# One more rounded chunk pair, its low part on GpSimd: a change to a fused attention and feed-forward kernel

## The chip, the cores and the metric

The kernel runs on one core of one Trainium2 chip. The metric is device time in microseconds (us) of one execution; lower is better. The engines of the core are named as the profile names them: PE (TensorE, matmuls), PEld (its weight loads), DVE (VectorE), ACT (ScalarE), POOL (GpSimd) and SP (SyncE, which here issues every DMA).

## The reference

Two stages in f32. First an attention through 49 "agents" per batch (4 batches of 12480 tokens, width 128): every agent takes a softmax over all keys and gathers values, then every token takes a softmax over the agents and gathers those. Then a feed-forward layer on the 49920 token rows that come out:

```python
h = x @ w_in            # 128 -> 2048
g = h - np.tanh(h)
return (g @ w_out)      # 2048 -> 128
```

## The kernel before

Tokens are cut into 100 blocks of up to 500 (the last of each batch has 480), 25 to a batch. The 2048 hidden columns are cut into 16 chunks of 128, taken two at a time: a block has 8 *chunk pairs*, i = 0 to 7, and one chunk pair of one block is a *step*. Two neighbouring blocks form a *block pair* of 16 steps; the step's place in it is its *position*, `pos = n % 2 * 8 + i`, 0 to 15. There are 800 steps in 50 block pairs, and nearly all the time goes into them.

A step consists of

- the first product on PE (`m1`, line 563): six matmuls into a PSUM tile h. The attention output is never formed; its 49 rows are folded into w_in beforehand;
- on ACT, y = tanh(h) (line 573) and z = a scaled square of y (line 578). Since h is small, h - tanh(h) is taken as h times that square;
- on DVE, the product g = h * z (`mul`, line 583), 128 x 1000, from PSUM and SBUF into SBUF;
- the second product (`m2`, line 632), which adds g times w_out into a PSUM tile acc of the block. It has two forms. The *plain* form multiplies g as f32 with an f32 copy of the weights (`wo_f`). The *rounded* form splits g in two numbers of the faster matmul type: GpSimd rounds it to gh (`high`, line 613), DVE subtracts to get the low part gl = g - gh (`low`, line 618), and PE does gh with the low weights, gh with the high weights and gl with the high weights, 12 matmuls of 500 columns in six pairs of row halves.

`PLAIN = (1, 3, 7, 8, 9)` lists the positions with the plain form; the first block is all plain. So 545 steps are rounded and 255 plain.

The order of the work on each engine is the order in which it is recorded (lines 850 to 915, `issue_order`): in step k come product k on DVE and its rounding on POOL; tanh and square of step k+1; the first product of step k+2; the low part of step k-1 (`low(1)` keeps one back); and the second product of step k-1 (`out`). An engine does its instructions strictly in that order. Position 2 also begins by closing the previous block: ACT copies half of acc to o (line 644), DVE adds the other half (line 641). The tiles g, gh and gl rotate over 4, 3 and 3 buffers; h, acc and small PSUM tiles share four double banks.

Between the steps lie smaller jobs. Each block pair prepares the token softmax of the next (lines 508 to 552). In the first three batches the first product over keys and values of the next batch (`phase1`) is handed out piece by piece from the queue `kq`: 13 score jobs, two for the maximum, 13 value jobs (marked by the table `VS`, starting at positions 1 and 8), then the rest. A value job has a subtraction on GpSimd (line 344).

After a block pair's second block is closed, one DMA of up to 1000 columns stores both (line 809).

Of the kernel before, what the change touches and what calls it, by code (L numbers as in the profile page):

```python
# [12 lines left out]
F32 = mybir.dt.float32  # L13
# [6 lines left out]
ALU = mybir.AluOpType  # L20
# [38 lines left out]
KV = 3  # L59
VB = 4  # L60
PLAIN = (1, 3, 7, 8, 9)
NB = dict(y=2, z=2, g=4, gh=3, gl=3)
Q0 = 2
NV = 10
# [9 lines left out]
VS = {1: 1, 8: 2}  # L74
# [4 lines left out]
def width(n):  # L79
    return min(BLK, N - n % NBLK * BLK)  # L80


def column(n):
    return n // NBLK * N + n % NBLK * BLK
# [18 lines left out]
class Build:  # L103
# [31 lines left out]
    def constants(self):  # L135
# [17 lines left out]
        self.wo_l = c.tile([128, NCH, C], F32R, tag="wo_l", name="wo_l")  # L153
        self.wo_f = {i: c.tile([128, 2 * C], F32, tag=f"wo_f{i}", name=f"wo_f{i}") for i in sorted({i % 8 for i in PLAIN})}
        self.vb = [c.tile([128, GT, C + 2], F32, tag=f"v{i}", name=f"v{i}") for i in range(VB)]
# [47 lines left out]
    def load_w_out(self, c, raw):  # L203
        one, two = self.wtile("gl", NB["gl"]), self.wtile("gh", NB["gh"])
        cut = lambda t, k: t[:, 512 * k : 512 * (k + 1)]
        return self.decode(raw, self.wf[:, c * 512 : (c + 1) * 512], cut(one, 0), cut(one, 1), cut(two, 0), cut(two, 1))
# [364 lines left out]
    def tanh(self, h, w):  # L571
        y = self.wtile("y", NB["y"])[:, : 2 * w]
        self.nc.scalar.activation(self.pair(y), h, AF.Tanh, scale=TSC)  # L573
        return y

    def square(self, y):
        z = self.wtile("z", NB["z"])[:, : y.shape[1]]
        self.nc.scalar.activation(z, y, AF.Square, scale=GSC)  # L578
        return z

    def mul(self, h, z, w):
        g = self.wtile("g", NB["g"])[:, : 2 * w]
        self.nc.vector.tensor_tensor(self.pair(g), h, self.pair(z), ALU.mult)  # L583
        self.mul_at = self.last_name()
        return g

    def act_general(self, hv, w):
        nc = self.nc
        d = self.wtile("y", NB["y"])[:, : 2 * w]
        u = self.wtile("z", NB["z"])[:, : 2 * w]  # L590
        nc.scalar.activation(self.pair(d), hv, AF.Tanh)
# [21 lines left out]
        self.nc.gpsimd.tensor_scalar(gh, g, 1.0, 0.0, ALU.mult, ALU.add)  # L613
        return gh

    def low(self, g, gh):
        gl = self.wtile("gl", NB["gl"])[:, : g.shape[1]].bitcast(F32R)
        self.nc.vector.tensor_tensor(gl, g, gh.bitcast(F32), ALU.subtract)  # L618
        return gl

    def m2(self, acc, i, gh, gl, wf=None):
        nc = self.nc
        w = gh.shape[1] // 2
        high, low = (lambda c: self.wo_h[:, 2 * i + c, :]), (lambda c: self.wo_l[:, 2 * i + c, :])
        if gl is None:
            terms = [(lambda c: wf[:, c * C : (c + 1) * C], gh, c) for c in range(2)]
        else:
            terms = [(low, gh, 0), (high, gh, 0), (low, gh, 1), (high, gh, 1), (high, gl, 0), (high, gl, 1)]
        for k, (weights, g, c) in enumerate(terms):
            for r in range(2):  # L630
                rows = slice(HALF * r, HALF * (r + 1))
                nc.tensor.matmul(  # L632
                    acc[:, r, :w],
                    weights(c)[rows],
                    g[rows, c * w : (c + 1) * w],
                    start=i == 0 and k == 0,
                    stop=i == NCH // 2 - 1 and k == len(terms) - 1,
                )
# [46 lines left out]
    def fast(self):  # L685
        nc, tc = self.nc, self.tc
        HP = NCH // 2
        blocks = [(b, j) for b in range(B) for j in range(NBLK)]
        steps = [(n, i) for n in range(len(blocks)) for i in range(HP)]
# [100 lines left out]
        kq = []  # L790
        r1, r2, done = [], [], []
# [7 lines left out]
        def out_at(n):  # L799
            first = n - n % 2  # L800
            if n == first and n // 2 not in outs:
                outs[n // 2] = self.work.tile([128, GW], F32, tag="out", name="o", bufs=2)
            return outs[n // 2][:, n % 2 * width(first) :][:, : width(n)]

        def finish(n):
            self.add_up(out_at(n), acc[n])
            if n % 2 == 1:
                w = width(n - 1) + width(n)
                nc.sync.dma_start(self.outT[:, column(n - 1) : column(n - 1) + w], outs[n // 2][:, :w])

# [13 lines left out]
        def product(k):  # L824
            n, i = steps[k]
            g = self.mul(hs.pop(k), zs.pop(k), width(n))
            plain = n == 0 or n % 2 * HP + i in PLAIN
            gh = None if plain else self.high(g)
            r1.append((n, i, g, gh))

        def low(keep):
            while len(r1) > keep:
                n, i, g, gh = r1.pop(0)
                r2.append((n, i, g, None) if gh is None else (n, i, gh, self.low(g, gh)))

        def out(k):
            while r2:
# [12 lines left out]
        for k, (n, i) in enumerate(steps):  # L850
            b = blocks[n][0]
            pos = (n % 2) * HP + i
            p = n // 2
            if n % NBLK == 0 and i == 0 and b + 1 < B:
                kq = self.phase1(b + 1)
            begin = kq[0][0].get(pos, 0) if kq and n else 0
            if done and done[0][1] < k - 1:
                self.take(out_at(done[0][0]), acc[done[0][0]])
                finish(done.pop(0)[0])
            product(k)  # L860
            if n == LATE and i < NP:
                self.bound(0, i, slice(PCUT[i], PCUT[i + 1]))
# [18 lines left out]
            for j in AHEADS.get(pos, (AHEAD,)) if n else (AHEAD,):  # L881
                first_product(k + j)
            low(1)
            mark = self.last_on(ET.DVE)
            if n == 0:
# [16 lines left out]
            for kind in [x[0] for x in kq[:begin]]:  # L902
                if kind is kq[0][0] and kind.get(pos):
                    start(kq.pop(0)[1](pos))
        low(0)
        out(len(steps))
        while done:
            self.take(out_at(done[0][0]), acc[done[0][0]])
            finish(done.pop(0)[0])
# [64 lines left out]
```

## Time and profile before

| | |
|---|---|
| time, 3 runs | 2016.40, 2017.02 (median), 2018.77 us |
| the profiled execution | 2018.59 us |
| its span, first to last instruction | 2016.8 us |
| busy in the span: PE, DVE, ACT, POOL | 1986.9, 1825.6, 1806.5, 999.9 us |
| mean granted TensorE clock | 0.995 of full |

A matmul's row in the profile covers its whole passage through the array, so neighbouring matmuls overlap; what a group of matmuls takes of PE's time is read from the distance between starts. Two matmuls of 64 rows each, on the two halves of the array, run side by side. Line numbers are those of the kernel before; in the changed kernel the same lines stand one further up to the storing of a block, and three to five further behind it.

### The profile page before, as it was taken

How to read it: one execution, taken by the hardware profiler on the slowest of the kernel's cores; microseconds unless marked ns; L12 is line 12 of the kernel's file. 1: busy time of each engine (PE TensorE's matmuls, PEld its weight loads, DVE VectorE, ACT ScalarE, POOL GpSimd, SP SyncE). 2: the span in 40 equal slices, each digit the busy share in tenths (PEclk: the TensorE clock that was granted, in tenths of full speed). 3: DMA queues.
4: the chain of work that ended last, by engine and by line, in shares of the span. 5: the costliest groups of instructions: out<-in, count | busy, mean ns of one | idle time of the engine just before them, and what ended most of it. 6: DMA issues, size and time to landing. Idle time of an engine off the chain costs nothing.

```text
span 2016.8 us, 49577 instructions
## 1 busy us (share of the span) xinstructions
PE 1986.9 (99%) x20779; PEld 1460.9 (72%) x20779; DVE 1825.6 (91%) x1986; ACT 1806.5 (90%) x2052; POOL 999.9 (50%) x702
## 2 busy tenths in 40 slices
PE   8899999999999999999999999999999999999998
PEld 7477767777677777777677777777767777777775
DVE  7799999889999998898999999889899999999997
ACT  3789989899999998899999999998999999999996
POOL 1254455555445455554454454555545546555554
PEclk9899999999999999999999999999999999999999
DMA  9422112221111222221012111221101101101100
GB/s 331 135 85 93 54 45 84 83 61 44 54 61 65 78 71 60 78 75 60 31 36 92 61 58 44 71 61 56 54 29 34 52 31 35 52 29 37 39 24 27
DMA packets 76601, 129.70 MB, mean 64 GB/s; under 512 B 5384, under 2 KB 55376, under 8 KB 76368
## 3 DMA queue, kind: packets, MB, share of 16 engines
q1 hardware_dynamic: 76368, 126.44, 19.2%
q8 instruction: 165, 2.70, 0.6%
q14 instruction: 68, 0.56, 0.1%
HBM read 81.10 MB, written 25.56 MB: 53 GB/s over the span
## 4 chain that ended last, share of the span: by engine, by line
PE 84%; ACT 8%; DVE 4%; issue 2%; DMA 1%; SPq 0%; POOL 0%; DVEq 0%; POOLq 0%
PE acc L632 49%; PE h L563 26%; ACT z L578 4%; ACT y L573 4%; DVE g L583 2%; PE misc L508 2%; PE misc L357 2%; PE pt L538 1%; PE misc L301 1%; PE h L273 1%; DVE gl L618 1%; PE misc L472 1%; DMA v<-w_out 1%; PE h L380 0%; ACT s L349 0%
## 5 line engine op out<-in xcount | busy, mean ns | idle before, releaser
L613 POOL TENSOR_SCALAR gh<-g 128x1000 fp32r<-128x1000 f32 (+1 forms) x545 | 853.0, 1565 | 622.5 <-DVE g L583 578.6
L583 DVE TENSOR_TENSOR g<-h,z 128x1000 f32<-128x1000 f32 (+1 forms) x800 | 955.5, 1195 | 133.5 <-ACT z L578 122.9
L573 ACT ACTIVATE y<-h 128x1000 f32<-128x1000 f32 (+1 forms) x800 | 802.4, 1003 | 68.6 <-PE h L563 60.5
L578 ACT ACTIVATE z<-y 128x1000 f32<-128x1000 f32 (+1 forms) x800 | 831.4, 1039 | 25.4
L618 DVE TENSOR_TENSOR gl<-g,gh 128x1000 fp32r<-128x1000 f32 (+1 forms) x545 | 656.8, 1205 | 1.3 <-POOL gh L613 1.0
L563 PE MATMUL h<-pT,awh 49*128 49x504 f32 x1600 | 552.0, 424 | 0.0
L632 PE MATMUL acc<-g,wo_f 64*128 64x500 f32 (+1 forms) x1960 | 443.3, 578 | 0.0
L632 PE MATMUL acc<-gh,wo_l 64*128 64x500 f32 (+1 forms) x2180 | 433.0, 387 | 0.5 <-POOL gh L613 0.2
L632 PE MATMUL acc<-gh,wo_h 64*128 64x500 f32 (+1 forms) x2180 | 432.6, 386 | 0.0
L563 PE MATMUL h<-pT,awl 49*128 49x504 f32 x800 | 369.5, 462 | 7.2 <-DVE awl L476 3.4
L632 PE MATMUL acc<-gl,wo_h 64*128 64x500 f32 (+1 forms) x2180 | 341.2, 387 | 1.0 <-DVE gl L618 0.5
L563 PE MATMUL h<-pb,awh 49*128 49x504 f32 x1600 | 317.1, 387 | 0.0
L563 PE MATMUL h<-pb,awl 49*128 49x504 f32 x800 | 309.0, 386 | 0.0
L632 PEld LDWEIGHTS acc<-g,wo_f 64*128 64x128 f32 x1960 | 190.6, 186 | 145.3 <-issue 126.1
L563 PEld LDWEIGHTS h<-pT,awh 49*128 49x128 f32 x1600 | 265.9, 186 | 20.9 <-issue 11.1
L632 PEld LDWEIGHTS acc<-gh,wo_h 64*128 64x128 f32 x2180 | 214.3, 186 | 37.2
L632 PEld LDWEIGHTS acc<-gl,wo_h 64*128 64x128 f32 x2180 | 211.5, 184 | 40.0 <-DVE gl L618 5.7
L632 PEld LDWEIGHTS acc<-gh,wo_l 64*128 64x128 f32 x2180 | 211.1, 184 | 38.6 <-POOL gh L613 1.7
L563 PEld LDWEIGHTS h<-pT,awl 49*128 49x128 f32 x800 | 147.6, 184 | 117.4 <-DVE o L641 49.9
L529 POOL TENSOR_TENSOR pp<-qe,pp 128x392 fp32r<-128x392 f32 x50 | 51.5, 1030 | 265.3 <-DVE pp L527 257.2
L563 PEld LDWEIGHTS h<-pb,awh 49*128 49x128 f32 x1600 | 153.9, 184 | 29.9 <-DMA pb<-pT 0.5
L563 PEld LDWEIGHTS h<-pb,awl 49*128 49x128 f32 x800 | 149.3, 187 | 11.7 <-issue 6.4
(113 smaller groups left out, 1130.4 us busy)
## 6 DMA issues: line engine op xcount, KB each, us to landing
kt<-kT SPq DMA_DIRECT2D x48, 512.0 KB
qt<-qT SPq DMA_DIRECT2D x46, 500.0 KB
outT<-o SPq DMA_DIRECT2D x46, 500.0 KB
pb<-pT SPq DMA_DIRECT2D x200, 96.5 KB
v<-v SPq DMA_DIRECT2D x36, 512.0 KB
vt<-v SPq DMA_DIRECT2D x12, 512.0 KB
raw<-w_in SPq DMA_DIRECT2D x4, 512.0 KB
v<-w_out SPq DMA_DIRECT2D x4, 512.0 KB
```

Source lines behind the costliest of these rows:

```text
L273: nc.tensor.matmul(ps[:, t // 4, (t % 4) * A2 : (t % 4 + 1) * A2], kt[:, t, :], self.ag[:, 0:2, :], start=True, stop=True,)
L301: nc.tensor.matmul(to, kt[:, t, r : r + QUART], self.ag[:, b, :], start=True, stop=True)
L357: nc.tensor.matmul(ps[HALF * odd : HALF * odd + w, : C + 1], flat[:r, t * A : t * A + w], vt[:r, t, : C + 1], start=t < 2, stop=t >= n - 2,)
L508: nc.tensor.matmul(to, qt[:, token : token + QUART], self.ag[:, b, :], start=True, stop=True)
L529: nc.gpsimd.tensor_tensor(pp[:, :, HALF:PW], ev, pp[:, :, :A].bitcast(F32), ALU.subtract)
L563: nc.tensor.matmul(h[:, c, : BT * TT], aw[a][rows[c], sl], pT[p][rows[c], :], start=k == 0, stop=k == 2)
L573: self.nc.scalar.activation(self.pair(y), h, AF.Tanh, scale=TSC)
L578: self.nc.scalar.activation(z, y, AF.Square, scale=GSC)
L583: self.nc.vector.tensor_tensor(self.pair(g), h, self.pair(z), ALU.mult)
L613: self.nc.gpsimd.tensor_scalar(gh, g, 1.0, 0.0, ALU.mult, ALU.add)
L618: self.nc.vector.tensor_tensor(gl, g, gh.bitcast(F32), ALU.subtract)
L632: nc.tensor.matmul(acc[:, r, :w], weights(c)[rows], g[rows, c * w : (c + 1) * w], start=i == 0 and k == 0, stop=i == NCH // 2 - 1 and k == ...
```

## The change

Three edits.

1. Position 1 changes from the plain to the rounded form, from the third block on, except where the next job in the queue is a value job, and its low part is made by GpSimd right after the rounding, not by DVE one step later.
2. The very last step of all (position 15 of the last block pair) changes from the rounded to the plain form.
3. The last two blocks are stored by a DMA each, when each is closed, in place of one DMA for both.

```diff
+POOL_LOW = (1,)
...
-    def low(self, g, gh):
+    def low(self, g, gh, pool=False):
         gl = self.wtile("gl", NB["gl"])[:, : g.shape[1]].bitcast(F32R)
-        self.nc.vector.tensor_tensor(gl, g, gh.bitcast(F32), ALU.subtract)
+        (self.nc.gpsimd if pool else self.nc.vector).tensor_tensor(gl, g, gh.bitcast(F32), ALU.subtract)
         return gl
...
             self.add_up(out_at(n), acc[n])
-            if n % 2 == 1:
+            if n >= len(blocks) - 2:
+                nc.sync.dma_start(self.outT[:, column(n) : column(n) + width(n)], out_at(n))
+            elif n % 2 == 1:
...
             g = self.mul(hs.pop(k), zs.pop(k), width(n))
-            plain = n == 0 or n % 2 * HP + i in PLAIN
+            pos = n % 2 * HP + i
+            pool = n > 1 and pos in POOL_LOW and not (kq and kq[0][0] is VS) and k < len(steps) - 1
+            plain = n == 0 or pos in PLAIN and not pool or k == len(steps) - 1
             gh = None if plain else self.high(g)
-            r1.append((n, i, g, gh))
+            r1.append((n, i, g, gh, self.low(g, gh, True) if pool else None))
 
         def low(keep):
             while len(r1) > keep:
-                n, i, g, gh = r1.pop(0)
-                r2.append((n, i, g, None) if gh is None else (n, i, gh, self.low(g, gh)))
+                n, i, g, gh, gl = r1.pop(0)
+                r2.append((n, i, g, None) if gh is None else (n, i, gh, gl or self.low(g, gh)))
```

In the built program 37 of the 49 block pairs after the first take edit 1 (the second products with the f32 weights of chunk pair 1 go from 98 to 61). What that does to the order of one ordinary block pair of the last batch is seen on two engines. On POOL, before, from the roundings of positions 14, 15 and 0 on; the next ones are of positions 2 and 4, then a part of the token softmax (qe):

```order
L613 TENSOR_SCALAR gh_24429<-g_24427 128x1000
L613 TENSOR_SCALAR gh_24458<-g_24456 128x1000
L613 TENSOR_SCALAR gh_24496<-g_24494 128x1000
L613 TENSOR_SCALAR gh_24562<-g_24560 128x1000
L613 TENSOR_SCALAR gh_24641<-g_24639 128x1000
L517 TENSOR_TENSOR qe_24644<-qe_24644,qm_24643 128x392
```

and the same place in the changed kernel, where the numbers of the tiles are others:

```order
L614 TENSOR_SCALAR gh_24314<-g_24312 128x1000
L614 TENSOR_SCALAR gh_24343<-g_24341 128x1000
L614 TENSOR_SCALAR gh_24381<-g_24379 128x1000
L614 TENSOR_SCALAR gh_24416<-g_24414 128x1000
L619 TENSOR_TENSOR gl_24418<-g_24414,gh_24416 128x1000
L614 TENSOR_SCALAR gh_24451<-g_24449 128x1000
L614 TENSOR_SCALAR gh_24538<-g_24536 128x1000
L518 TENSOR_TENSOR qe_24541<-qe_24541,qm_24540 128x392
```

The rounding and the low part of position 1 (gh_24416, gl_24418) now stand between the roundings of positions 0 and 2. DVE's order is the same in both kernels.

On PE, before, from the low terms of position 0 to the token scores (misc) that follow the second product of position 1:

```order
L632 MATMUL acc_24544<-gl_24542,wo_h_84 128x500 x4
L563 MATMUL h_24568<-pT_24368,awl_20245 128x504
L563 MATMUL h_24568<-pT_24368,awh_20244 128x504 x2
L563 MATMUL h_24568<-pb_24369,awl_20245 128x504
L563 MATMUL h_24568<-pb_24369,awh_20244 128x504 x2
L632 MATMUL acc_24544<-g_24529,wo_f1_87 128x500 x4
L508 MATMUL misc_24581<-ag_67,qt0_99 32x49 x32
```

and in the changed kernel:

```order
L633 MATMUL acc_24433<-gl_24431,wo_h_84 128x500 x4
L564 MATMUL h_24457<-pT_24253,awl_20533 128x504
L564 MATMUL h_24457<-pT_24253,awh_20532 128x504 x2
L564 MATMUL h_24457<-pb_24254,awl_20533 128x504
L564 MATMUL h_24457<-pb_24254,awh_20532 128x504 x2
L633 MATMUL acc_24433<-gh_24416,wo_l_85 128x500 x2
L633 MATMUL acc_24433<-gh_24416,wo_h_84 128x500 x2
L633 MATMUL acc_24433<-gh_24416,wo_l_85 128x500 x2
L633 MATMUL acc_24433<-gh_24416,wo_h_84 128x500 x2
L633 MATMUL acc_24433<-gl_24418,wo_h_84 128x500 x4
L509 MATMUL misc_24478<-ag_67,qt1_100 32x49 x32
```

The four f32 matmuls (eight instructions in the trace) have become eight with gh and four with gl; the four with gl are the last before the scores, and read what GpSimd makes.

At the end of the program, PE before:

```order
L632 MATMUL acc_26687<-gl_26827,wo_h_84 128x480 x4
L632 MATMUL acc_26687<-gh_26825,wo_l_85 128x480 x2
L632 MATMUL acc_26687<-gh_26825,wo_h_84 128x480 x2
L632 MATMUL acc_26687<-gh_26825,wo_l_85 128x480 x2
L632 MATMUL acc_26687<-gh_26825,wo_h_84 128x480 x2
L632 MATMUL acc_26687<-gl_26841,wo_h_84 128x480 x4
```

and in the changed kernel, from the last matmuls of position 14:

```order
L633 MATMUL acc_27131<-gh_27248,wo_l_85 128x480 x2
L633 MATMUL acc_27131<-gh_27248,wo_h_84 128x480 x2
L633 MATMUL acc_27131<-gl_27270,wo_h_84 128x480 x4
L633 MATMUL acc_27131<-g_27268,wo_f7_89 128x480 x4
L926 MATMUL misc_27293<-ident_69,bm_27291 1x128
```

The last rounded second product has become one of four f32 matmuls, which wait for g alone; the last rounding and low part are gone from POOL and DVE.

## The prediction

> **What bounds the kernel now.** I read the page's busy shares first, then a window of one whole block pair of the last batch, which has no jobs for a next batch, from one store of the output to the next.
>
> ```profile
> PE 1986.9 (99%) x20779; PEld 1460.9 (72%) x20779; DVE 1825.6 (91%) x1986; ACT 1806.5 (90%) x2052; POOL 999.9 (50%) x702
> 1828.38:1865.27 36.89, 36.89 (x350) 27.84 (x348) 34.01 (x36) 34.98 (x39) 19.59 (x13) 1.00 0.12 40
> ```
>
> PE is never idle in those 36.89 us; DVE is busy 34.01 (third of the busy times), ACT 34.98, POOL 19.59. So PE sets the pace, but the others have only 2 to 3 us a block pair to spare, and only POOL has real room. Then the chain of waits in a stretch of ordinary steps, for what each form of the second product takes of PE (start, length, what):
>
> ```profile
> 602.41 1.36 PE acc L632 x12
> 609.26 1.68 PE acc L632 x8
> 629.04 1.68 PE acc L632 x8
> ```
>
> Rounded 1.36 us, plain 1.68. The change takes 0.32 us from PE at position 1 and pays with GpSimd, on which nothing waits much. What decides is when GpSimd's low part arrives. So last the timeline of positions 0 to 3, where the change falls. Columns: start, length, engine, line, operation.
>
> ```profile
> 1822.84 1.19 DVE L583 TENSOR_TENSOR g<-h,z 128x1000 f32<-128x1000 f32 x1
> 1824.22 1.83 POOL L613 TENSOR_SCALAR gh<-g 128x1000 fp32r<-128x1000 f32 x1 [0.41 <-DVE g L583]
> 1825.06 1.19 DVE L583 TENSOR_TENSOR g<-h,z 128x1000 f32<-128x1000 f32 x1
> 1826.17 1.19 DVE L618 TENSOR_TENSOR gl<-g,gh 128x1000 fp32r<-128x1000 f32 x1
> 1828.27 1.19 DVE L583 TENSOR_TENSOR g<-h,z 128x1000 f32<-128x1000 f32 x1
> 1829.20 1.84 PE L632 MATMUL acc<-g,wo_f 64*128 64x500 f32 x8
> 1829.65 1.03 POOL L613 TENSOR_SCALAR gh<-g 128x1000 fp32r<-128x1000 f32 x1 [3.60 <-DVE g L583]
> 1829.66 1.20 DVE L583 TENSOR_TENSOR g<-h,z 128x1000 f32<-128x1000 f32 x1 [0.19 <-ACT z L578]
> 1830.77 1.19 DVE L618 TENSOR_TENSOR gl<-g,gh 128x1000 fp32r<-128x1000 f32 x1
> 1830.97 0.90 PE L508 MATMUL misc<-ag,qt 128*32 128x49 f32 x64
> 1831.88 1.19 DVE L583 TENSOR_TENSOR g<-h,z 128x1000 f32<-128x1000 f32 x1
> 1832.59 0.40 PE L632 MATMUL acc<-gh,wo_l 64*128 64x500 f32 x2
> 1833.50 0.63 PE L632 MATMUL acc<-gl,wo_h 64*128 64x500 f32 x4
> 1833.95 0.39 PE L563 MATMUL h<-pT,awh 49*128 49x504 f32 x1
> 1834.91 1.20 DVE L583 TENSOR_TENSOR g<-h,z 128x1000 f32<-128x1000 f32 x1 [1.37 <-ACT z L578]
> ```
>
> The DVE products are those of positions 0 (1822.84), 1 (1825.06), 2, 3, 4 (1831.88) and 5 (1834.91). Only 0 and 2 are followed by a rounding on POOL. Position 1 is plain, and its f32 matmuls start on PE at 1829.20, 2.95 us after their product ended at 1826.25: it was ready long before. The rows at 1832.59, 1833.50 and 1833.95 are the rounded second product of position 2 and what follows it: 0.91 us of gh terms, then 0.45 of gl terms, 1.36 together.
>
> **The change part by part: the low part on GpSimd.** Count: 37 positions, each with one rounding and one subtraction more on POOL, twelve matmuls in place of four, and DVE as before. GpSimd has no subtraction of 1000 columns in the trace; its two-input operations are
>
> ```profile
> L214 POOL TENSOR_TENSOR wo_l<-awh,wo_h x4: 1274/1294/1487, 78.7 to 90.1; 128x512 fp32r<-128x512 f32 x4
> L529 POOL TENSOR_TENSOR pp<-qe,pp x50: 1022/1028/1125, 46.5 to 1957.3; 128x392 fp32r<-128x392 f32 x50
> L517 POOL TENSOR_TENSOR qe<-qe,qm x50: 836/844/1088, 37.4 to 1944.9; 128x392 f32<-128x392 f32 x50
> L344 POOL TENSOR_TENSOR s<-s,mb x39: 400/959/1853, 287.4 to 1431.2; 128x392 f32<-128x392 f32 x36, 128x98 f32<-128x98 f32 x3
> ```
>
> (shortest, median, longest in ns). L214 is the very same subtraction, f32 less its rounded copy, on 512 columns. From 392 columns (1.022 us) to 512 (1.274) is 2.1 ns a column; 488 more make 1.274 + 1.025 = 2.30 us. Low bound: the two with a broadcast operand, 0.836 us at 392 and 0.400 at 98, give 1.48 ns a column and 1.74 us. High bound: 1.028 us scaled in proportion, 2.62. I take 2.30, since the nearest row is the same operation.
>
> Beside a DVE low part a rounding takes 1.83 us (at 1824.22, over DVE's gl), alone 1.03 (at 1829.65, beside a product, which reads PSUM). Now the walk. Product 1 ends at 1826.25. The rounding follows 0.19 later, as at 1824.03 to 1824.22, falls on DVE's low part of position 0 (1826.17), and so takes 1.83: 1826.44 to 1828.27. The subtraction waits for it on its own engine, which I put at 0.10, half of that hand-over: 1828.37 to 1830.67. Beside it DVE has only products and the closing of a block, which read PSUM. PE starts the gh terms at 1829.20 as now and wants gl 0.91 later, at 1830.11. It gets it at 1830.67 and 0.06 for the hand-over (as POOL to PE at the end of the program, below), 1830.73: **PE waits 0.62 us**, and has the gl terms done 0.45 later, at 1831.18. Before, the scores followed at 1830.97. So each changed position costs 0.21 us, where without a wait it would gain: end at 1830.56, that is 0.41 (0.32 by the chain). PE can't do something else meanwhile: scores, first product 5 and second product 2 are queued behind the waiting matmul.
>
> It is a loop that no head start dissolves: product 1 depends on a first product that PE itself made three steps before the second product, and everything since stands in line on ACT, DVE and POOL. And it is alike all over the program. The first changed block pair:
>
> ```profile
> 110.07 1.20 DVE L583 TENSOR_TENSOR g<-h,z 128x1000 f32<-128x1000 f32 x1
> 114.23 1.84 PE L632 MATMUL acc<-g,wo_f 64*128 64x500 f32 x8
> ```
>
> Product to second product 2.96 us, the 2.95 of above. So 37 x 0.21 = **+7.8 us**. With the low bound of 1.74 the wait is 0.06 and each position gains 0.35, -13.0 us; with 2.62 it is +0.53, +19.6 us.
>
> [...]
>
> **What is late next.** Rounding 2 now waits for POOL: 1830.67 to 1831.70 instead of 1829.65. Low part 2 on DVE follows it, 1831.74 to 1832.93, instead of 1830.77; PE wants it at 1833.50 + 0.21, so it is in time. Product 4 is queued behind it on DVE: about 1832.9 to 1834.1 instead of 1833.07. First product 6 needs the PSUM tile that product 4 frees, and comes at 1833.95 + 0.21 = 1834.16: just in time. DVE's 1.37 us of idleness before product 5 takes up the rest. I cost this at nothing; if that cover is gone, every 0.1 us of wait at first product 6 is 3.7 us.
>
> **The end of the program.**
>
> ```profile
> 1994.32 1.78 PE L632 MATMUL acc<-g,wo_f 64*128 64x480 f32 x8
> ...
> 2004.81 1.73 POOL L613 TENSOR_SCALAR gh<-g 128x960 fp32r<-128x960 f32 x1 [0.40 <-DVE g L583]
> 2005.75 0.70 PE L632 MATMUL acc<-gl,wo_h 64*128 64x480 f32 x4
> 2006.60 0.49 PE L632 MATMUL acc<-gh,wo_l 64*128 64x480 f32 x2
> 2007.79 0.71 PE L632 MATMUL acc<-gl,wo_h 64*128 64x480 f32 x4
> 2009.82 0.34 SPq L809 DMA_DIRECT2D outT<-o  x1
> ```
>
> The last rounded step ends on PE at 2007.79 + 0.71 = 2008.50. In f32 it can follow position 14 at 2005.75 + 0.45 = 2006.20 and takes 1.78: 2007.98, **-0.5 us**. The closing stays. The last store halves from 490 KB to 245:
>
> ```profile
> 2010.80:2011.80 1.00, 0.00 (x0) 0.00 (x0) 0.00 (x0) 0.00 (x0) 0.00 (x0) 1.00 0.93 353
> ```
>
> At 353 GB/s, the last number, 245 KB are 0.7 us; the fixed part stays, so I take **-0.5** (bounds 0 and -0.7). The earlier store of block 98 goes out a block sooner, on an SP queue with nothing behind it.
>
> **Sum.** +7.8 - 0.5 - 0.5 = +6.8 us, 0.34%. The profiled execution took 2018.59, so 2025.4 by its own time; it was 1.57 above the median of 2017.02, and by that the forecast is **2023.8**.
>
> **The rivals.** What a measurement of this kernel can tell from no change is about 0.2%, 4 us: below 2013.0 is faster, above 2021.1 slower.
>
> *The low part arrives in time*: GpSimd does 1000 columns in 1.74 us or less, as the broadcast rows would have it, and PE gains 0.33 to 0.41 at each position: 2017.02 - 1.0 - 37 x 0.33 to 0.41, 2001 to 2004, up to 2013 with a part of the wait. Against it: the same subtraction at 512 columns takes 1.27. This is the case on the other side, and it turns where the subtraction takes 2.09 us. 0.13.
>
> *It cancels*: 2.0 to 2.15 us, by the bare proportion of the row of 0.844; -0.09 to +0.06 a position, 2013 to 2018. 0.15.
>
> *A second wait behind the first*: hand-overs of 0.1 or 0.2 more, or a rounding 2 that falls on a DVE operation, push product 4 past first product 6, whose margin is 0.02 us. 0.1 to 0.3 more a position, 3.7 to 11.1 us: 2027.5 to 2035. For it speaks the margin, against it the 1.37 us of idleness. 0.15.
>
> *The change moves nothing on the path*: ACT, at 34.98 of 36.89 us, would have to be the true bound, and hold the time whatever PE does. Within 0.2%; PE without an idle slice speaks against it. 0.02.
>
> *The forecast*: a subtraction of 2.15 to 2.45 us, +0.06 to +0.36 a position, 2018 to 2029. 0.55.
>
> **How the numbers follow.** Slower: the forecast without its lowest fifth or so, 0.45, and the second wait, 0.15: 0.60. Within 0.2%: cancelling 0.14, the forecast's low end 0.10, nothing moved 0.02: 0.26. Faster: 0.14. The range of 2012 to 2033 leaves out most of the low part in time and the worst of the second wait, some 0.18; the likeliest case's own is 2018 to 2029.
>
> **What would show it.** In the trace after: POOL subtractions at 2.3 us (below 2.1 I am wrong in sign); PE waiting some 0.6 us for POOL's gl in each of the 37 (the wait may hide in a longer matmul row); a block pair of the last batch at 37.1 us instead of 36.89; DVE idle before low part 2, and product 5 no later than PE is. If block pairs shrink to 36.5, the low part was in time; if they grow past 37.3, look at first product 6. At the end, PE done 0.5 us sooner after its last position 14, and a last store of 245 KB.

## The result, and the profile after

The changed kernel takes 2037.51 us (median; 2036.95 to 2040.35), the kernel before beside it 2017.89 (2016.4 to 2019.36): ratio 1.01, 95% interval 1.0083 to 1.0118. It is slower, as forecast, but by 19.6 us instead of 6.8, and outside the range of 2012 to 2033. The profiled execution's span grew from 2016.8 to 2038.5 us, by 21.7: the traced execution of the changed kernel was the longest of its four, so the traces lie 2 us further apart than the medians.

The profile page of the kernel after has its busy times and its chain by engine (the chain of work that ended last, as shares of the span):

```profile
PE 1988.0 (98%) x20923; PEld 1480.5 (73%) x20923; DVE 1827.8 (90%) x1985; ACT 1806.6 (89%) x2052; POOL 1148.9 (56%) x775
PE 75%; ACT 9%; POOL 8%; DVE 5%; issue 2%; DMA 1%; SPq 0%; POOLq 0%; DVEq 0%
```

PE is about as busy as before, in a span that is 21.7 us longer, and POOL is on the chain with 8% where it had 0%. The view of waits (us in total, times, longest in us) and the group of the new subtraction (shortest, median, longest in ns):

```profile
PE acc L633 <- POOL gl L619: 18.2, 37, 0.6
DVE gl L619 <- POOL gh L614: 32.9, 38, 1.0
L619 POOL TENSOR_TENSOR gl<-g,gh x37: 2262/2352/2367, 112.7 to 1998.2; 128x1000 fp32r<-128x1000 f32 x35, 128x960 fp32r<-128x960 f32 x2
```

PE's wait stands in all 37 positions; its 0.49 us each count from the end of the matmul row before. The second row is DVE standing idle before low part 2, 0.9 us a position, which the prediction named as a sign. The subtraction takes 2.35 us where I had put 2.30. One of the positions in the timeline, in the last batch:

```profile
1845.74 1.19 DVE L584 TENSOR_TENSOR g<-h,z 128x1000 f32<-128x1000 f32 x1
...
1847.11 1.83 POOL L614 TENSOR_SCALAR gh<-g 128x1000 fp32r<-128x1000 f32 x1 [0.39 <-PE acc L633]
...
1849.02 2.35 POOL L619 TENSOR_TENSOR gl<-g,gh 128x1000 fp32r<-128x1000 f32 x1
...
1849.86 0.39 PE L633 MATMUL acc<-gh,wo_l 64*128 64x500 f32 x2
...
1851.42 0.72 PE L633 MATMUL acc<-gl,wo_h 64*128 64x500 f32 x4 [0.49 <-POOL gl L619]
...
1852.07 0.90 PE L509 MATMUL misc<-ag,qt 128*32 128x49 f32 x64
...
1852.40 1.20 DVE L619 TENSOR_TENSOR gl<-g,gh 128x1000 fp32r<-128x1000 f32 x1 [0.88 <-POOL gh L614]
...
1853.51 1.19 DVE L584 TENSOR_TENSOR g<-h,z 128x1000 f32<-128x1000 f32 x1
```

Product 1, its rounding, the subtraction to 1851.37. The second product of position 1 begins at 1849.86; its low terms could start 0.91 later, at 1850.77, and start at 1851.42; the scores follow at 1852.07. From the second product's start to the scores that is 2.21 us; before it was 1.77 (1829.20 to 1830.97). So a position costs 0.44 us, and a block pair of the last batch takes 37.3 us instead of 36.9 or the predicted 37.1. Product 4 (1853.51) comes 0.97 us later than its place; product 5 gives 0.53 of it back, and there is no second wait at first product 6.

**Where the 21.7 us are.** I compared the times of the 800 products of the two traces, block pair by block pair. The 37 changed ones grew by 0.45 us in the median, the unchanged ones by 0.0; five of them by much more (3.73, 1.50, 1.37, 2.31 and 1.49 us), one by twice as much, two shrank. In sum, to about 0.2 us: 37 x 0.45 = 16.6; 6.0 more in the outliers but one (the two that shrank counted in); 1.1 in that one; the first product 0.6 earlier; the end of the program 1.35 shorter (PE done 0.43 sooner after its last position 14, the last store 0.9). 16.6 + 6.0 + 1.1 - 0.6 - 1.35 = 21.7.

**The outliers.** In the largest one the timeline of PE shows a stop in the midst of one stream of small matmuls, with nothing waited for:

```profile
236.55 0.90 PE L509 MATMUL misc<-ag,qt 128*32 128x49 f32 x64
237.27 0.82 PE L302 MATMUL misc<-ag,kt 128*32 128x49 f32 x57
239.63 0.29 PE L302 MATMUL misc<-ag,kt 128*32 128x49 f32 x7 [1.54 <-issue]
```

and behind it, in a view by stretches (length, busy time of PE, PEld, DVE, ACT, POOL, then the granted clock, the busy share of the DMA engines and GB/s), a clock that falls to half for about 3.4 us and costs the rest of this block pair's 3.73 us:

```profile
239.60:241.00 1.40, 1.37 (x17) 1.16 (x18) 0.51 (x2) 1.02 (x3) 0.70 (x1) 1.00 0.64 209
241.00:242.00 1.00, 1.00 (x10) 0.82 (x8) 0.83 (x2) 0.97 (x2) 0.84 (x1) 0.57 0.61 152
242.00:243.00 1.00, 1.00 (x8) 0.85 (x6) 0.05 (x1) 0.91 (x1) 0.00 (x0) 0.50 0.83 328
243.00:244.00 1.00, 1.00 (x8) 0.78 (x8) 1.00 (x1) 0.00 (x0) 0.00 (x0) 0.50 0.06 25
244.00:245.00 1.00, 1.00 (x6) 0.48 (x4) 1.00 (x2) 0.80 (x1) 0.69 (x1) 0.72 0.00 0
```

Six such stops stand in the trace after (0.5 to 1.9 us from one instruction's start to the next), two in the one before (0.8 and 0.9). Only the one at 239.6 us has a slow clock behind it. The experiments had two questions: what makes 0.45 of the predicted 0.21, and what the stops are.

### The profile page after: what moved, and what is told of

The parts are those of the page before. It is cut to its first block, busy times and chain, and to the rows that moved or that the text cites. A ratio compares the mean times of both kernels' runs of the same rounds, so it can differ in the third digit from the quotient of the medians.

```text
span 2038.5 us, 49973 instructions
## 1 busy us (share of the span) xinstructions
PE 1988.0 (98%) x20923; PEld 1480.5 (73%) x20923; DVE 1827.8 (90%) x1985; ACT 1806.6 (89%) x2052; POOL 1148.9 (56%) x775
## 3 DMA queue, kind: packets, MB, share of 16 engines
q8 instruction: 166, 2.72, 0.5%
## 4 chain that ended last, share of the span: by engine, by line
PE 75%; ACT 9%; POOL 8%; DVE 5%; issue 2%; DMA 1%; SPq 0%; POOLq 0%; DVEq 0%
PE acc L633 43%; PE h L564 23%; POOL gl L619 4%; ACT z L579 4%; ACT y L574 4%; POOL gh L614 3%; DVE g L584 2%; PE misc L509 2%; PE misc L358 2%; PE pt L539 1%; PE misc L302 1%; PE h L274 1%; DVE gl L619 1%; PE misc L473 1%; ACT s L350 0%
## 5 line engine op out<-in xcount | busy, mean ns | idle before, releaser
L614 POOL TENSOR_SCALAR gh<-g 128x1000 fp32r<-128x1000 f32 (+1 forms) x581 | 916.5, 1578 | 490.0 <-DVE g L584 428.7
L633 PE MATMUL acc<-gh,wo_l 64*128 64x500 f32 (+1 forms) x2324 | 462.9, 387 | 0.3
L633 PE MATMUL acc<-gh,wo_h 64*128 64x500 f32 (+1 forms) x2324 | 462.7, 386 | 0.0
L633 PE MATMUL acc<-gl,wo_h 64*128 64x500 f32 (+1 forms) x2324 | 368.9, 391 | 19.4 <-POOL gl L619 18.2
L633 PE MATMUL acc<-g,wo_f 64*128 64x500 f32 x1672 | 377.9, 578 | 0.0
L633 PEld LDWEIGHTS acc<-gl,wo_h 64*128 64x128 f32 x2324 | 223.9, 185 | 73.5 <-POOL gl L619 33.8
L633 PEld LDWEIGHTS acc<-gh,wo_h 64*128 64x128 f32 x2324 | 230.1, 186 | 39.0
L633 PEld LDWEIGHTS acc<-g,wo_f 64*128 64x128 f32 x1672 | 166.4, 186 | 123.8 <-issue 107.8
L633 PEld LDWEIGHTS acc<-gh,wo_l 64*128 64x128 f32 x2324 | 226.8, 184 | 39.9 <-POOL gh L614 1.1
```

Of the source, the lines that this page charges most:

```text
L633: nc.tensor.matmul(acc[:, r, :w], weights(c)[rows], g[rows, c * w : (c + 1) * w], start=i == 0 and k == 0, stop=i == NCH // 2 - 1 and k == ...
```

## The experiments

The ratios are to the kernel before, run beside them (medians 2016.97 to 2017.96).

**1. The end alone.** `POOL_LOW = ()`: position 1 stays plain, the last position and the two last stores are changed.

> The changed kernel without its first edit: position 1 stays plain everywhere, only the last step is plain and the last two blocks are stored apart. Theory A (the whole loss comes from position 1, where PE waits for GpSimd's low part; in the changed trace the two edits at the end gave back 0.4 us on PE and 0.9 us after the last store): 1.3 us less than before, about 2016.6, not to be told from no change by the times, but to be seen at the end of the trace. Rival: the edits at the end, by the other program that they make, carry a part of the loss of 20 us: 2020 or more.

2018.24 us, ratio 1.0003 (0.9993 to 1.0012). Behind the first block pair, which was 0.8 us longer, none grew by over 0.1 us, and the one with the stop at 222.5 us lost that stop, though TensorE's program is the same up to there. In the trace the last data landed 1.5 us sooner after the product of position 14 (11.5 us instead of 13.0), but the program ended 4.2 us behind it instead of 2.5, so this span shows no gain at the end, and the times don't either. The end is not what made it slower.

**2. A low part that comes early.**

```diff
-        (self.nc.gpsimd if pool else self.nc.vector).tensor_tensor(gl, g, gh.bitcast(F32), ALU.subtract)
+        if pool:
+            self.nc.gpsimd.tensor_scalar(gl, gh.bitcast(F32), 2.0 ** -14, 0.0, ALU.mult, ALU.add)
+        else:
+            self.nc.vector.tensor_tensor(gl, g, gh.bitcast(F32), ALU.subtract)
```

> The changed kernel, but GpSimd makes position 1's low part by an operation with one input (gh times a constant) in place of the subtraction; the subtraction is left out, so the low part's values are others. Matmuls, order and buffers are as in the changed kernel. One-input operations of 1000 columns take 1.03 us on GpSimd where nothing disturbs them, the subtraction 2.35. Theory A (PE's wait for the 2.35 us is the loss): the low part comes at 1849.02 + 1.03 + 0.05 = 1850.10 where PE wants it at 1850.77, no wait, and each of 37 positions gains 0.32 to 0.41 us: 2001 to 2005. Rival B (the rounded form at position 1 costs it whatever makes the low part, by a busier GpSimd or by other neighbours of the f32 matmuls): 2015 or more.

2007.40 us, ratio 0.9949 (0.9932 to 0.9966), 2.4 above the expected range: the wait was the cost, and without it the rounded position pays. The timeline of the same place:

```profile
1820.65 1.03 POOL L620 TENSOR_SCALAR gl<-gh 128x1000 fp32r<-128x1000 f32 x1
...
1821.50 0.39 PE L636 MATMUL acc<-gh,wo_l 64*128 64x500 f32 x2
...
1822.42 0.62 PE L636 MATMUL acc<-gl,wo_h 64*128 64x500 f32 x4
...
1822.97 0.90 PE L509 MATMUL misc<-ag,qt 128*32 128x49 f32 x64
```

1.47 us from the second product's start to the scores, 0.30 less than the plain one. I had 0.41: the last four matmuls take 0.55 to the scores, not the 0.45 that they take to a first product.

**3. TensorE takes low part 1 later**, behind position 2's second product; GpSimd's order as in the change.

```diff
+                if isinstance(gl, tuple):
+                    self.m2(acc[n], i, gh, None, part=1)
+                    late.append((n, i, gl[1], k))
+                    continue
...
+            while late and late[0][3] < k:
+                n, i, gl, _ = late.pop(0)
+                self.m2(acc[n], i, None, gl, part=2)
```

> The changed kernel, but PE does the low terms of position 1 one step later, after the second product of position 2; GpSimd's order stays. Theory A1 (only PE's wait for the low part costs, and what is late behind it on GpSimd and VectorE is hidden): each position gains 0.32 to 0.41, 2001 to 2005. Theory A2 (the delay behind it counts as soon as PE is not itself late: rounding 2 waits for the subtraction, low part 2 for that, product 4 is 0.97 us late and first product 6 needs its PSUM tile): PE waits 0.5 to 0.6 us at first product 6 in place of the wait removed, net +0.1 to +0.2 a position, 2021 to 2025.

2021.66 us, ratio 1.002 (1.001 to 1.003). TensorE no longer waits for the subtraction, but rounding 2 stands behind it on GpSimd, and product 4 behind low part 2 on VectorE; product 4 is 0.98 us late and first product 6 waits for it:

```profile
1834.73 1.19 DVE L584 TENSOR_TENSOR g<-h,z 128x1000 f32<-128x1000 f32 x1
...
1835.97 0.18 PEld L564 LDWEIGHTS h<-pT,awl 49*128 49x128 f32 x1 [0.36 <-DVE g L584]
```

The product ends at 1835.92. Just before, TensorE also waits 0.23 us for low part 2: the matmuls with it start at 1834.87 instead of 1834.64. The wait that the prediction had as a rival was there once the first one was gone.

**4. The subtraction behind rounding 2 and VectorE's low part 2**, TensorE's four matmuls behind position 3's second product.

> Position 1 rounded in the same 37 block pairs, but GpSimd subtracts only after its rounding 2 and after VectorE's low part 2 have gone by, and PE does the low terms two steps later, after the second product of position 3. Both A1 and A2: no wait is left, rounding 2 and product 4 come when they came before, each position gains 0.32 to 0.41 us: 2001 to 2005. Rival (ScalarE at 35.0 and VectorE at 34.0 of 36.9 us a block pair take over as soon as PE has less to do): gain under 0.2 a position, 2010 to 2016.

2014.35 us, ratio 0.9984 (0.9975 to 0.9994): better than before, but only 0.18 us a changed block pair of the 0.30 of experiment 2. The time is the rival's; its reason, ScalarE and VectorE as the bound, is not what the timeline shows. There is a new collision:

```profile
1828.57 2.35 POOL L619 TENSOR_TENSOR gl<-g,gh 128x1000 fp32r<-128x1000 f32 x1 [1.44 <-PE h L564]
...
1830.88 1.04 POOL L614 TENSOR_SCALAR gh<-g 128x1000 fp32r<-128x1000 f32 x1
...
1831.87 0.86 POOL L518 TENSOR_TENSOR qe<-qe,qm 128x392 f32<-128x392 f32 x1
...
1831.95 1.83 DVE L619 TENSOR_TENSOR gl<-g,gh 128x1000 fp32r<-128x1000 f32 x1 [0.16 <-POOL gh L614]
```

The subtraction ends at 1830.92 and makes rounding 4 late; so the softmax's subtraction falls on VectorE's low part 4, which takes 1.83 us instead of 1.19, and product 6 is some 0.9 us late.

**5. What are the stops?** The changed kernel with 128 more TensorE instructions at 34 us (the token scores of block pair 0 twice).

```diff
-        for t in range(GT):
+        for t in list(range(GT)) * (2 if self.nq == 1 else 1):
```

> The changed kernel with the token-score matmuls of block pair 0 issued twice (64 more matmuls and 64 more weight loads of TensorE at about 34 us; the second pass writes the same numbers again). Theory P: TensorE's long stops without a releaser ('issue' of 0.5 us and more: 222.5 and 1143.1 us before; 239.6, 704.1, 721.2, 1078.0, and two of 0.5 us at 1182.5 and 1199.6 after) come where the next 16 KB packet of the instruction queue has not been there long enough. In every trace so far the instruction that such a stop ends with has a count, over TensorE's recorded weight loads, matmuls and sequencer instructions, that leaves 193 when divided by 256 (5057 and 25025 before; 5569, 15553, 16065, 22977 after; 5569 in three of the experiments; 16384 B / 256 = 64 B), and a packet of that queue landed 1.3 to 1.5 us ahead of it. 128 more instructions ahead move every such boundary by half a page: the stops at 240, 704, 721, 1078, 1183 and 1200 us are gone, and new ones can stand only where 256 consecutive instructions take under about 3.4 us in the changed trace and a shifted boundary ends them: at about 143, 159, 624, 640 and 1104 us. The remainder stays 193. The time: 0.7 to 1.5 us for the added matmuls if they are on the path, the stops about the same in sum: 2034 to 2041 us. Rival Q: the stops belong to the places (a transfer that arrives late, a throttle): they stay at 240, 704, 721 and 1078 us within 3 us.

2039.16 us, ratio 1.01 (1.0085 to 1.0115). All six stops are gone, the block pairs that had grown by 3.73, 1.50, 1.37 and 2.31 grew by 0.47, 0.49, 0.44 and 0.48 like the others, and new stops stand at 147, 165, 628 and 645 us (said: about 143, 159, 624 and 640; the one at 1104 did not come). One of them:

```profile
144.80 1.04 PE L302 MATMUL misc<-ag,kt 128*32 128x49 f32 x78
147.29 0.36 PE L302 MATMUL misc<-ag,kt 128*32 128x49 f32 x10 [1.45 <-issue]
```

Counted over TensorE's recorded instructions (weight loads, matmuls, sequencer), the instruction that ends a stop was

```
kernel        count of the instruction (us)                                              count mod 256   packet landed before it
before        5057 (222.5), 25025 (1143.1)                                               193             1.45, 1.48 us
after         5569 (239.6), 15553 (704.1), 16065 (721.2), 22977 (1078.0),
              25793 (1182.5), 26305 (1199.6)                                             193             1.28 to 1.43 us
after + 128   3009 (147.3), 3521 (164.8), 13505 (627.8), 14017 (644.8)                   193             1.26 to 1.45 us
```

The packets are those of one row of the DMA view (packets, MB):

```profile
q8 instruction: 166, 2.72, 0.5%
```

2.72 MB in 166 packets are 16 KB each, and 42,145 instructions in 256 a packet are 165. From these numbers and the table I take it that one packet holds 256 of TensorE's instructions, and call them a page; that is an estimate from the counts. With packets and pages taken in order, no page was entered less than 1.45 us after its packet landed in the trace before, and none less than 1.28 us in the trace after. The packet was asked for within 2 us of the entry into the page before, ahead of it or behind it, in 92% and 90% of the pages. The eight stops of these two traces follow pages that took 1.84 to 3.06 us without the stop (the 3.4 us of the expectation were an estimate). But TensorE didn't stand after every such page: the kernel before entered pages at 238.9, 578.0 and 594.9 us after 2.45, 1.84 and 3.26 us in the one before, without a stop. The change put 8 instructions more into each of 37 positions, and with them other instructions on the pages' edges. Theory P holds for the places of the stops, Q is out. The time did not fall. In the trace the new stops took 4.4 us where the old had taken 7.6, but the first product came 2.2 us later; over the 14 traces it comes at 60.8 to 65.3 us, so that isn't shown to be the added matmuls.

**6. How the cost follows the lateness:** two one-input operations in place of the subtraction.

```diff
+            self.nc.gpsimd.tensor_scalar(gl, gh.bitcast(F32), 2.0 ** -14, 0.0, ALU.mult, ALU.add)
+            self.nc.gpsimd.tensor_scalar(gl, gh.bitcast(F32), 2.0 ** -14, 0.0, ALU.mult, ALU.add)
```

> The changed kernel with the subtraction of position 1 on GpSimd replaced by two one-input operations of about 1.03 us each (both write a constant multiple of the rounded value, so the true low part of these 37 positions is left out). Theory A: what the change costs is how late the low part reaches TensorE: 1.03 us gave -0.30 us a position, 2.35 us gives +0.44 us. Two operations take 2.06 us, so the wait falls from 0.65 to about 0.35 us, and a position costs +0.14 us: 37 x 0.30 = 11 us less than the changed kernel, 2025 to 2029 us. Rival C: the cost comes with the subtraction's two inputs (what it does to VectorE and ScalarE beside it), not with its lateness: 2006 to 2011 us, as with one operation.

2031.71 us, ratio 1.0062 (1.0047 to 1.0076); a position cost 0.27 us.

```profile
1843.98 1.04 POOL L620 TENSOR_SCALAR gl<-gh 128x1000 fp32r<-128x1000 f32 x1
...
1844.82 0.39 PE L637 MATMUL acc<-gh,wo_l 64*128 64x500 f32 x2
...
1845.11 1.05 POOL L621 TENSOR_SCALAR gl<-gh 128x1000 fp32r<-128x1000 f32 x1
...
1846.21 0.71 PE L637 MATMUL acc<-gl,wo_h 64*128 64x500 f32 x4 [0.32 <-POOL gl L621]
...
1846.85 0.90 PE L509 MATMUL misc<-ag,qt 128*32 128x49 f32 x64
```

The low part ends at 1846.16, 0.69 us ahead of the scores; in the changed kernel it was 0.70 (1851.37 to 1852.07). So the cost goes with the lateness (A), not with the second input (C). The number of the expectation missed by 3 us: with the gap between them the two operations take 2.18 us, not 2.06, 0.17 less than the subtraction, and a position fell by 0.18.

**7. Another position, taken late.** `POOL_LOW = (7,)`, where GpSimd is idle for 6 us, with the late matmuls of experiment 3.

> The kernel before with its end as in the changed kernel, position 1 plain again, and position 7 rounded instead (34 positions, where no value jobs head the queue): GpSimd, which stands idle there for over 6 us in the last batch, makes the low part; TensorE takes the low part's four matmuls after position 8's second product, so that they are 1.7 us later than their place. Theory A: position 7's saving on TensorE is the 0.30 us that the run without a wait showed, nothing waits for GpSimd, and the products behind have 2.8 us of slack: 34 x 0.30 = 10 us, less 1 us at the end, plus 1 to 4 us of issue stops: 2006 to 2011 us. Rival D: at positions 8 to 10 ScalarE and VectorE set the pace (the softmax of the next block pair lies there), so TensorE's earlier end turns into a wait: 2014 to 2018 us.

2062.28 us, ratio 1.0221 (1.0208 to 1.0235), a miss of both theories. Position 7 ends a block, and the late matmuls are the last of its sum: the closing waits for them. In the waits, ACT's closing for PE rose from 20.0 us to

```profile
ACT o L649 <- PE acc L637: 68.1, 50, 5.3
PE h L564 <- DVE o L646: 47.5, 35, 1.4
```

ACT and DVE stand in their order behind the closing, the first product behind DVE: 1.3 us in each changed block pair.

**8. VectorE makes low part 1**, in its usual place; the rest as in the change.

```diff
-            r1.append((n, i, g, gh, self.low(g, gh, True) if pool else None))
+            r1.append((n, i, g, gh, None))
```

> The changed kernel with the low part of position 1 made by VectorE in its usual place (behind product 2) in place of GpSimd. Theory A (only the lateness counts): product 2 ends some 0.6 us after GpSimd's rounding of position 1, VectorE's subtraction takes 1.19 us, so the low part is there at about the time at which TensorE wants it (0 to 0.2 us late); TensorE saves 0.1 to 0.3 us a position: 2006 to 2014 us. Rival E: VectorE becomes the bound, since a product and a low part are 2 x 1.19 = 2.38 us against 2.30 us a position of TensorE: the 1.19 us are missing further on, a wait of TensorE for a product of VectorE takes the place of the one for GpSimd, and the time is 2018 us or more.

2030.62 us, ratio 1.0062 (1.0047 to 1.0076); a position cost 0.33 us.

```profile
1845.96 0.39 PE L633 MATMUL acc<-gh,wo_l 64*128 64x500 f32 x2
...
1846.14 1.19 DVE L619 TENSOR_TENSOR gl<-g,gh 128x1000 fp32r<-128x1000 f32 x1
...
1847.39 0.71 PE L633 MATMUL acc<-gl,wo_h 64*128 64x500 f32 x4 [0.34 <-DVE gl L619]
...
1848.03 0.90 PE L509 MATMUL misc<-ag,qt 128*32 128x49 f32 x64
```

The same wait with another engine's name: low part 1 ends at 1847.33, again 0.70 us ahead of the scores. I had it at most 0.2 us late; TensorE started the low terms 0.5 us late (1847.39 instead of 0.91 behind 1845.96). The time is E's, but its reason, VectorE as a bound further on, isn't what the trace shows.

**9. The subtraction in two halves**: 500 columns behind rounding 1, 500 behind rounding 2 and low part 2, in the gap that plain position 3 leaves on GpSimd; TensorE's four matmuls behind position 3's second product.

```diff
+    def half(self, gl, g, gh, c):
+        w = g.shape[1] // 2
+        at = slice(c * w, (c + 1) * w)
+        self.nc.gpsimd.tensor_tensor(gl[:, at], g[:, at], gh[:, at].bitcast(F32), ALU.subtract)
...
+                self.half(gl, g, gh, 0)
...
+                self.half(gl, g, gh, 1)
+                self.wait_for(at, name)
```

> The changed kernel with GpSimd's subtraction of position 1 cut into two halves of 500 columns (about 1.25 us each): the first right behind rounding 1, the second behind rounding 2 and VectorE's low part of position 2, in the gap that position 3 (plain, no rounding) leaves on GpSimd; TensorE takes the four matmuls of low part 1 behind position 3's second product. Theory A: what the mended order lost to (the subtraction's end at 1830.92 us, into rounding 4 and the softmax's subtraction) is gone, since the second half ends 1.1 us earlier; nothing waits for GpSimd, and every changed position gives the 0.30 us that the one-operation run gave: 37 x 0.30 = 11 us less, 1 us at the end, 5 to 7 us of issue stops as in the runs with the same number of TensorE instructions, against 1.6 us before: 2006 to 2011 us. Rival F: rounding 2 is late by the first half (about 0.5 us) and VectorE's low part of position 2 with it, so product 4 is late as in the run with the late terms: 2012 to 2020 us.

**2008.20 us, ratio 0.9954 (0.9940 to 0.9968)**: faster than both kernels, with the whole computation in it.

```profile
1820.78 1.28 POOL L625 TENSOR_TENSOR gl<-g,gh 128x500 fp32r<-128x500 f32 x1
...
1822.06 1.04 POOL L614 TENSOR_SCALAR gh<-g 128x1000 fp32r<-128x1000 f32 x1
...
1822.65 0.90 PE L509 MATMUL misc<-ag,qt 128*32 128x49 f32 x64
...
1823.21 1.19 DVE L619 TENSOR_TENSOR gl<-g,gh 128x1000 fp32r<-128x1000 f32 x1
...
1824.48 1.27 POOL L625 TENSOR_TENSOR gl<-g,gh 128x500 fp32r<-128x500 f32 x1 [1.39 <-DVE gl L619]
...
1825.73 1.03 POOL L614 TENSOR_SCALAR gh<-g 128x1000 fp32r<-128x1000 f32 x1
```

Rounding 2 and rounding 4 (1822.06, 1825.73) both take their 1.03 us, low part 2 its 1.19, and TensorE waits for none of them. A changed block pair is 0.29 us shorter than before in the median, though this program has five of the stops (5.3 us).

**10. Position 7, in halves, taken in its usual place.** `POOL_LOW = (7,)`, both halves behind the rounding.

> The kernel before with its end as in the changed kernel, position 1 plain again, and position 7 rounded (34 positions); the low part by GpSimd in two halves directly behind its rounding, TensorE's terms in their usual place, so that the closing of the block is no longer behind them (in the run with position 7's terms late, ScalarE waited 68.1 us in 50 closings for them). Theory A: the rounding ends at about 1842.5 us of the trace before, the halves at 1843.8 and 1845.0, wanted at 1844.75 and 1844.97: a wait of 0.1 us at most; TensorE saves 0.2 to 0.3 us a position: 7 to 10 us, 1 us at the end, less 1 to 4 us of issue stops: 2006 to 2013 us. Rival D: ScalarE and VectorE set the pace at positions 8 to 10, and TensorE's earlier end turns into a wait there: 2014 to 2020 us.

2018.59 us, ratio 1.0006 (0.9997 to 1.0015); the block pairs changed by 0.0.

```profile
1844.67 2.50 POOL L625 TENSOR_TENSOR gl<-g,gh 128x500 fp32r<-128x500 f32 x2
...
1846.57 0.40 PE L642 MATMUL acc<-gh,wo_h 64*128 64x500 f32 x2
...
1846.79 0.92 PE L642 MATMUL acc<-gl,wo_h 64*128 64x500 f32 x4
...
1847.22 0.19 PEld L642 LDWEIGHTS acc<-gl,wo_h 64*128 64x128 f32 x2 [0.45 <-POOL gl L625]
...
1847.55 1.84 PE L642 MATMUL acc<-g,wo_f 64*128 64x500 f32 x8
```

The second half ends at 1847.17, in the midst of the four low matmuls; the last two of them want it, and the loading of their weights waits for it. The four take 0.92 us instead of 0.62. The second product of position 7 takes 1.67 us (1845.88 to 1847.55), the plain one took 1.68: a lateness of about 0.2 us eats the whole saving. That is again the price of being late, and not D's pace of the other engines, though the time is D's.

**11. Positions 1 and 7, both in halves.**

> Both: position 1 as in the run with halves, position 7 as in the run with position 7 in halves. If the two gains stand beside each other they add: 1997 to 2006 us. If GpSimd (some 60% busy then) or VectorE becomes the bound of a stage, the time stays at or above the better of the two.

**2003.66 us, ratio 0.9933 (0.9920 to 0.9947)**, the fastest. But block pair by block pair it is like experiment 9 (-0.31 in the median). What differs are the stops: 8 more instructions for each rounded position 7 put other instructions on the edges, and two stops (14529 and 15041, 1.85 us) stand where experiment 9 had five (5.3 us). So the gain over experiment 9 is put down to where its pages happen to end; that is read from one trace of each kernel.

**12. The same 128 instructions in the kernel before.** The edit of experiment 5.

> The kernel before with the token-score matmuls of block pair 0 issued twice (64 more matmuls and weight loads of TensorE, 128 instructions, at about 34 us), nothing else. Theory P: the kernel before has only two long issue stops because few of its page boundaries (every 256 TensorE instructions, remainder 193) end a stretch in which 256 instructions go in under 3.4 us; with the boundaries moved by half a page seven do, by the trace of before: at about 143 us (2.3 us for 256 instructions), 159 (2.3), 657 (1.8), 673 (3.3), 1064 (2.7), 1169 (3.1) and 1206 (3.1), which will be the instructions 3009, 3521, 14529, 15041, 22977, 25793 and 26817 of the new program. At least three of these stops stand in the trace, those at 222.5 and 1143.1 us are gone, and the time is 2 to 8 us above before: 1 to 2 us for the added matmuls, 1 to 6 us of stops. So some 5 us of the changed kernel's 20 us would belong to no edit of it but to the count of its instructions. Rival Q: stops like these come only with the longer program of the rounded position (its wait for GpSimd): at most the two old stops, 0 to 2 us above before.

2019.14 us, ratio 1.0010 (1.0001 to 1.0019), 2.1 us above before and at the low end of what P gave. The two old stops are gone; of the seven named instructions two had a clear stop:

```profile
656.63 0.50 PE L563 MATMUL h<-pb,awh 49*128 49x504 f32 x2 [0.43 <-issue]
...
1063.99 0.28 PE L301 MATMUL misc<-ag,kt 128*32 128x49 f32 x4 [0.43 <-issue]
```

They are 14529 and 22977, both as named; a third, 3009, stood 0.2 us; the others passed. So the count says where a stop can stand, but at the same edges the program of before stood for less time than the longer one (3009: 0.2 us, 1.65 in experiment 5; 22977: 0.6, 1.9 in the changed kernel). At 704.1 and 1078.0 us of the changed kernel the next packet was asked for 1.1 and 2.3 us after the page before was entered; in the row at 656.63 it was asked for 0.1 us ahead. What decides that, I have not found out; it can differ between two executions of the same instructions, since 5057 had a stop in the kernel before and none in experiment 1, where its packet was asked for 0.5 us ahead of the entry instead of 0.65 behind it. That 5 us belong to the count alone, as the expectation had it, is therefore not shown: the edges come from the count, the length from something else as well.

## Why the prediction was wrong

**Right: the sign and the mechanism.** PE waits for GpSimd's low part at position 1, until 0.65 us after it could have started, against 0.62 predicted; the subtraction takes 2.35 us against 2.30, its start behind the rounding 0.08 against 0.10; the scores are behind the wait; product 4 slips by 0.97 against 1.0, and DVE's idleness ahead of product 5 takes it up, so the second wait did not come. The end gave 1.35 us against 1.0 in this trace (in that of experiment 1 it gave nothing).

**Wrong, first: the price of the last four matmuls behind the wait.** The step "has the gl terms done 0.45 later, at 1831.18" took the 0.45 from position 2, where a first product follows. Here token scores follow, and PE starts from a stand: from the low part's end to the scores it is 0.69 to 0.70 us in three kernels (experiments 6 and 8 and the change), against the 0.06 + 0.45 that I had. About half of the difference is the other neighbour (0.55 to the scores without a wait, experiment 2), half the start from a stand (0.64 to 0.65 with one). That makes 0.19 us a position, and with 0.05 for the later end of the subtraction, 0.21 becomes 0.45: 37 x 0.24 = 9 us of the miss. The same step is in the gain without a wait, 0.41 predicted, 0.30 and 0.29 measured (experiments 2 and 9). A plain row that ends in the same neighbour, 1829.20 to 1830.97, was in the prediction; the rounded one should have been carried over to that neighbour. That the measured 19.6 us equal the +19.6 of the prediction's high bound is chance: there the subtraction was to take 2.62 us, and it took 2.35. And where the prediction said to look at first product 6 if block pairs grow past 37.3 us, the excess was in these four matmuls instead.

**Wrong, second: nothing in the sum for the program's length.** Six issue stops, one with a slow clock behind it, took 7.6 us of the block pairs, the two of before 1.6: 6.0 us net in these two traces. That their places go with the instruction count is shown by experiment 5; what sets how long each lasts stays open (experiment 12). The two stops of before, each with its "issue" in the timeline, were not asked where they would go. Ahead of the stop at 239.6 us one stream issued 128 instructions, 64 weight loads and 64 matmuls, in 0.72 us (236.55 to 237.27); the stops of the trace after were 0.5 to 1.9 us from start to start, those of the trace before 0.8 and 0.9.

**Wrong, third, and small: a late rounding on GpSimd.** One block pair grew by 1.49 us without a stop of PE. There a rounding on GpSimd began 0.29 us late: it is GpSimd's instruction 324, and it started 0.44 us after the one before it instead of 0.15. So the rounding behind it fell on VectorE's low part:

```profile
536.63 2.02 POOL L614 TENSOR_SCALAR gh<-g 128x1000 fp32r<-128x1000 f32 x2 [1.05 <-DVE g L584]
...
537.69 2.01 DVE L619 TENSOR_TENSOR gl<-g,gh 128x1000 fp32r<-128x1000 f32 x1 [0.24 <-POOL gh L614]
```

2.01 us instead of 1.20. In experiment 6, with other counts on GpSimd, this block pair grew like its neighbours. The count of the late instruction, 324, leaves 68 when divided by 128, like those of 196 and 580, which started 0.42 and 0.41 us after the ones before them; that these are edges of pages too is my guess from the counts, and not shown.

The rivals: the low part in time would have been worth 37 x 0.30, less than its 0.33 to 0.41, and experiment 2 shows that it was the right mechanism; "it cancels" is what position 7 does (experiment 10); the second wait exists, but only when the first is taken away (experiment 3).

## What to carry to other kernels

Price an operand that may be late by two numbers from the same neighbourhood, the time from its arrival to the next instruction of the waiting engine and the time without a wait: here 0.70 and 0.55 us, and a lateness of 0.2 us was enough to eat a saving of 0.30. A slow operation on an idle engine can be cut and put into the gaps of that engine's own order, if its consumer is moved behind them (experiment 9: 0.29 us less a changed block pair) and isn't the last of a sum that others wait for (experiment 7: 1.3 us more). When a change adds or removes instructions on an engine that runs long streams of tiny ones, compare stage by stage and look for stops without a releaser before a few microseconds are put down to the edit (here 7.6 us in the trace after, 1.6 in the one before).

## What I had not expected of the hardware

In all twelve stops of the table in experiment 5 the instruction that ended the stop came 1.26 to 1.48 us after its 16 KB packet had landed. After a stop of 1.54 us the granted clock was at 0.50 for some 3.4 us (241.1 to 244.6), and so it was in experiment 6 after one of 1.93 us (1075.2 to 1078.6). But after one of 1.65 us in the changed kernel (1078.0) it stayed at 1.00, as it did after one of 0.87 us (704.1), and there the block pairs lost nothing beyond the stop. So the length of the stop alone does not decide it. What does is not shown here.
